# Block-sparse attention and a gated feed-forward on one core: the scores move between the two row tiles of the second product

## The chip, the core and the metric

The kernel runs on one core of one Trainium2 chip. The metric is the time of one execution on the device, in microseconds (us), as the median of several runs; lower is better. TensorE multiplies matrices and writes to PSUM; VectorE (DVE), ScalarE (ACT) and GpSimd (POOL) work elementwise; SyncE (SP) issues DMAs. Each engine takes its instructions in the order in which the program gives them.

## The reference

Inputs are q, k and v of 4 batches, 8 heads, 768 positions and head size 64, a table of three sampled key blocks for each of 24 query blocks, and two weight matrices, 512 by 2048 and back. Attention is masked by blocks of 32 positions; its output, 3072 rows of 512, goes through the feed-forward.

```python
scores = scale * np.matmul(q, k.transpose(0, 1, 3, 2))
mask = np.abs(blk_i - blk_j) <= window
mask = mask | (blk_i == 0) | (blk_j == 0) | (blk_i == n_blocks - 1) | (blk_j == n_blocks - 1)
...
scores = np.where(mask, scores, -1000000000.0)
attn = np.exp(scores - np.max(scores, axis=-1, keepdims=True))
attn = attn / (np.sum(attn, axis=-1, keepdims=True) + 1e-09)
x = np.matmul(attn, v)                      # then heads side by side: 3072 x 512
h = x @ w_in
sp = np.maximum(h, 0.0) + np.log1p(np.exp(-np.abs(h)))
g = h * erf(sp)
return g @ w_out
```

## The kernel before

Precision is kept by splitting: float32 values become two float16 halves, high and low, and a product is three float16 matmuls; the scores alone are float32 matmuls.

Attention is cut into 64 units, 16 for each batch: ten of kind "m" (a tile of four query blocks by half of the heads, with five key blocks and the sampled ones), four of kind "f" (the first and last query blocks, all keys) and two of kind "e" (the second and the one before the last query block). The feed-forward is cut into 96 groups: for each batch three chunks of two row tiles (u = 0 and 1, of 128 rows each), and for each chunk eight groups of 256 of the 2048 hidden columns.

The main loop runs over m, one step for each feed-forward group and two more. A step does, for its own group, the first product (`ff_first`, tile `h`, 24 matmuls of 128x256); for the unit two units back, where that completes a tile of rows, the values (`values`, tile `po`, 96 small matmuls, or 192 for the "f" and "e" units together); for a new unit the scores (`scores`, tiles `s_m`, `s_f`, `s_e`); and for the group two steps back the second product (`ff_second`, tile `o`, six matmuls of 128x512 for each row tile u). A table `until` spreads the 60 units left for the loop over its steps, so 60 of the 98 steps have a unit.

Around these, VectorE does `ff_gate` of the group one step back (tiles `q` and `g`), `norm` (`rinv`, `xf`), `soft_max` of the unit (the row maximum `mx`, then `nb`), `ff_power` and, late in the step, `soft_low` (`p`); ScalarE does `ff_logs` (`x`, `q`), the exponentials `soft_exp` (`pf`), `ff_exp`, and copies. `soft_turn` transposes the probabilities `p` into `pT` by a DMA in SyncE's queue; the same queue gathers the value rows (`vb`), loads queries and keys and writes results. GpSimd gathers the sampled key blocks (`keys`).

Buffers that order the work: one PSUM buffer for scores (`ps_s`), so scores of a unit wait for the exponentials of the unit before; one for `po`; three for `h`; two for `o`, so at a chunk's first group `ff_second` waits for the copies of the chunk before (`ff_store`, tile `wo<-o`: ScalarE for u = 0, VectorE for u = 1).

In the first steps the output weights are still being split into halves, by steps that short strings name (`EARLY`, `AMID`, `LATE`): `Ao` and `Bo` take a sum over the output weights for their scale (`top_wo`, then `whole_wo` on TensorE), `Ho0` and `Lo0` make the first high and low halves on ScalarE and VectorE, `Hi5` and the like those of the input weights. `EARLY[2]` is "Ao Bo Ho0 Lo0", in the step that is also the first with a second product. The scheduler keeps every engine's instructions in program order (`keep_in_program_order`). The profile gives all of them one line, L59, which is the wrapper that records them, so they are told apart by their tiles.

Of the kernel before, what the change touches and what calls it, by code (L numbers as in the profile page):

```python
# [42 lines left out]
def sparse_attention_moe(ctx: ExitStack, tc: tile.TileContext, qT, kT, v, sampled, w_in, w_out, out):  # L43
# [37 lines left out]
    FF_LAG = 2  # L81
# [25 lines left out]
    def key_blocks(b):  # L107
        return keys[:, b % 2 * (NB + 1) : (b % 2 + 1) * (NB + 1)]
# [134 lines left out]
    def write_values():  # L243
        for write in writes:
            sp.dma_start(*write)
        writes.clear()
# [318 lines left out]
    def near_keys(b, i, rows, pr):  # L565

        c = slice(pr * BLOCK, (pr + 1) * BLOCK)
        first = b % 2 * (NB + 1) + i - 1
        near = keys[rows, first : first + NR, c]
        apart = (kgs[b, i] - first) * HP * BLOCK  # L570
        return bass.AP(near.tensor, near.offset, [near.ap[0], (apart, 2), near.ap[1], near.ap[2]])
# [3 lines left out]
    def scores(unit):  # L575
        kind, b, n = unit[0], unit[1], unit[2:]
        tag = "_".join(str(x) for x in unit)
        s = ps_s.tile([P, 1024], F32, tag="s", name=f"s_{tag}")
        q = qts[b, n[0] if kind == "m" else MT]
        both = [slice(a * D, (a + 1) * D) for a in range(2)]  # L580

        def blocks_of(rows, pr, start, stop, step=1):
            return key_blocks(b)[rows, start:stop:step, pr * BLOCK : (pr + 1) * BLOCK]

        if kind == "f":
            (pr,) = n
            for c, e in ((0, 512), (512, S)):
                for rows in both:
                    k = blocks_of(rows, pr, c // BLOCK, e // BLOCK)
                    pe.matmul(s[rows, c:e], q[rows, pr, 2 * BLOCK :], k, start=True, stop=True)  # L590
            softs[unit] = (s[:, :S], 1, S)
            return
        if kind == "m":
            t, quad = n
            s4 = s.rearrange("p (a r w) -> p a r w", a=2, r=2)
            first, count, turns = 1 + 4 * t, 4, [(r, 0, s4[:, :, r]) for r in range(2)]
            softs[unit] = (s, 4, 256)
        else:
            (quad,) = n
            s3 = s.rearrange("p (a w) -> p a w", a=2)[:, :, :256]  # L600
            first, count, turns = NB - 3, 2, [(r, r * D, s3) for r in range(2)]
            softs[unit] = (s3, 2, 256)
        for r, o, out in turns:
            pr = 2 * quad + r
            for a, rows in enumerate(both):
                k = blocks_of(rows, pr, 0, NB, NB - 1)
                pe.matmul(
                    out[o : o + count * BLOCK, a, 192:], q[rows, pr, : count * BLOCK], k, start=True, stop=True
                )
        for r, o, out in turns:  # L610
            pr = 2 * quad + r
            for j in range(count):
                c = j * BLOCK
                for a, rows in enumerate(both):
                    place = out[o + c : o + c + BLOCK, a, :192]
                    near = near_keys(b, first + j, rows, pr)
                    pe.matmul(place, q[rows, pr, c : c + BLOCK], near, start=True, stop=True)
# [71 lines left out]
    CT = 2  # L689
# [14 lines left out]
    def ff_first(b, ch, fg):  # L704
        tag = f"{b}_{ch}_{fg}"
        isg = first_scale(b)
        h = ps_h.tile([P, W], F32, tag="h", name=f"h_{tag}")
        xT = xTs[b, ch].rearrange("p n u c -> p n (u c)")
        for j in range(FG):
            f = fg * FG + j  # L710
            hj = h[:, j * CW : (j + 1) * CW]
            for kt in range(NK):
                i, c = (f // 4) * NK + kt, (f % 4) * P
                hi, lo = wi16[:, i, c : c + P], wi16[:, i, 512 + c : 512 + c + P]
                xa, xb = xT[:, kt], xT[:, NK + kt]
                pe.matmul(hj, hi, xa, start=kt == 0, stop=False)
                pe.matmul(hj, hi, xb, start=False, stop=False)
                pe.matmul(hj, lo, xa, start=False, stop=kt == NK - 1)
        ffs[b, ch, fg] = (h, isg)
# [3 lines left out]
    def ff_logs(b, ch, fg):  # L723

        h, isg = ffs[b, ch, fg]
        tag = f"{b}_{ch}_{fg}"
        x = mo.tile([P, W], F32, tag="x", name=f"x_{tag}")
        act.activation(x, h, AF.Relu, bias=H_CAP, scale=isg)
        act.activation(x, x, AF.Exp, bias=H_CAP, scale=-1.0)
        act.activation(x, x, AF.Ln, bias=1.0, scale=C0)  # L730
        q = mo.tile([P, W], F32, tag="s", name=f"q_{tag}", bufs=2)
        act.activation(q, x, AF.Square, bias=C2)
        act.activation(x, x, AF.Ln, bias=1.0, scale=C4)
        ffs[b, ch, fg] = (h, x, q)
# [18 lines left out]
    def ff_second(b, ch, fg, u):  # L753
        if fg == 0:
            outs[u] = ps_o.tile([P, DM], F32, tag="o", name=f"o_{b}_{ch}_{fg}_{u}")
        g = gs[b, ch, fg]
        o = outs[u]
        for j in range(FG):
            f = fg * FG + j
            c = j * CW + u * P  # L760
            hi, lo = wo16[:, f, :512], wo16[:, f, 512:]
            pe.matmul(o, g[:, 0, c : c + P], hi, start=f == 0, stop=False)
            pe.matmul(o, g[:, 0, c : c + P], lo, start=False, stop=False)
            pe.matmul(o, g[:, 1, c : c + P], hi, start=False, stop=f == NF - 1)
# [21 lines left out]
    def write_results():  # L786
        for result in results:
            sp.dma_start(*result)
        results.clear()
# [71 lines left out]
    def seen(unit):  # L861

        if unit[0] == "m":
            return unit[1:]
        if unit[0] == "f" and unit[2] % 2 == 1:
            return unit[1], MT, unit[2] // 2
        return None

    def used_keys(unit):
        nonlocal kfree  # L870
        if unit[0] == "m" and unit[3] == 1:
            kfree += 4
        elif unit[0] == "e" and unit[2] == 1:
            kfree += 4
# [6 lines left out]
    def unit_of(n):  # L881
        return units[n] if 0 <= n < len(units) else None

    def values_of(place):
        nonlocal vfree
        values(*place)
        if place[2] == 1:
            vfree += 4 if place[1] < MT else 5
# [99 lines left out]
    groups = [(b, ch, fg) for b in range(B) for ch in range(NCH) for fg in range(NGR)]  # L988
    until = (12, 20, 25, 31, 36, 41, 47, 52, 57, 63, 67)
    for m in range(len(groups) + FF_LAG):  # L990
        ch, i = divmod(m, NGR)
        steps = 0
        if ch < len(until):
            first = until[ch - 1] if ch else FIRST
            steps = first + -(-(until[ch] - first) * (i + 1) // NGR) - begun
        elif begun < len(units) + PV_LAG:
            steps = 1
        assert steps in (0, 1)
        group = groups[m] if m < len(groups) else None
        last = groups[m - 1] if 0 < m <= len(groups) else None  # L1000
        unit = unit_of(begun) if steps else None
        old = unit_of(begun - PV_LAG) if steps else None
        place = seen(old) if old and begun - PV_LAG >= FIRST else None
        begun += steps
        write_values()
        write_results()
        if group:
            ff_first(*group)
            ff_logs(*group)
        if place:  # L1010
            values_of(place)
        if steps:
            gathers(begun)
        if unit:
            scores(unit)
            used_keys(unit)
        if last:
            ff_gate(*last)
        if place:
            norm(*place)  # L1020
        if m < len(EARLY):
            work(EARLY[m])
        if m >= FF_LAG:
            for u in range(CT):
                ff_second(*groups[m - FF_LAG], u)
        if unit:
            soft_max(unit)
            next_queries(begun - 1)
        if group:
            ff_power(*group)  # L1030
        if unit:
            soft_exp(unit)
        if group:
            ff_exp(*group)
        if m < len(AMID):
            work(AMID[m])
        if m >= FF_LAG:
            for u in range(CT):
                ff_store(*groups[m - FF_LAG], u)
        if place:  # L1040
            turn(*place)
        if unit:
            soft_low(unit)
            soft_turn(unit)
        if m < len(LATE):
            work(LATE[m])
        if unit:
            behind(begun - 1)
# [37 lines left out]
```

## Time and profile before

| | |
|---|---|
| median of 3 runs | 828.74 us (826.76 to 829.26) |
| profiled execution | 831.7 us, its span 829.9 us |
| TensorE busy | 698.5 us, 84% of the span |
| VectorE, ScalarE, GpSimd busy | 570.1, 551.3, 126.8 us |
| second product, 1152 matmuls | 385 ns each |
| mean granted clock of TensorE | 0.962 of full speed |

The profile is one execution. The loop's first step starts at about 96 us of the span, its last units' scores run near 732 us, and the rest is feed-forward alone. A busy share says how much an engine did in a stretch; what a change is worth there is told by the timeline, in which each row has the start and length of instructions that follow one another and, in brackets, how long the engine was idle before and for whom. Matmuls overlap, so the distance from one block's start to the next is used here instead of a block's own length.

### The profile page before, as it was taken

The page shows a single profiled execution, that of the slowest core. Times are in us where ns is not written, and L with a number is a line of the kernel's source. Part 1 is how long each engine was busy: PE and PEld are TensorE (multiplying, and loading weights), DVE is VectorE, ACT ScalarE, POOL GpSimd, SP SyncE. Part 2 cuts the span into 40 slices and gives each one's busy share as a digit, 9 for nine tenths or more (in the row PEclk, how much of TensorE's full clock was granted, in tenths as well). Part 3 has the DMA queues.
Part 4 walks back from the last instruction along what each step waited for, and adds up shares of the span by engine and source line. Part 5 has one row for each costly group of instructions (what it writes and reads, how often), then busy time and mean ns, then how long its engine had stood idle before and what let it go on. Part 6 is the DMA issues. An engine that isn't in the chain of part 4 may idle for free. (4 is left out here: it accounts for less than half of the span.)

```text
span 829.9 us, 26567 instructions
## 1 busy us (share of the span) xinstructions
PE 698.5 (84%) x10844; PEld 460.2 (55%) x10844; DVE 570.1 (69%) x987; ACT 551.3 (66%) x943; POOL 126.8 (15%) x343
## 2 busy tenths in 40 slices
PE   1254546888986879999999988999999999999997
PEld 1133423555654647566666556666666665666664
DVE  3994696787865666885668766876677767754454
ACT  4654567987755656776668657767677676675774
POOL 4621131002222121100103231000111110000000
PEclk9999767999998999999999999999999999999999
DMA  8999963887799898773598898752688858220000
GB/s 306 289 267 295 250 164 66 164 182 196 176 197 199 215 207 185 162 167 47 134 206 193 171 223 201 177 96 45 162 192 175 182 103 184 44 53 16 1 26 26
DMA packets 199930, 131.59 MB, mean 159 GB/s; under 512 B 144000, under 2 KB 167168, under 8 KB 199808
## 3 DMA queue, kind: packets, MB, share of 16 engines
q1 hardware_dynamic: 196384, 118.10, 62.5%
q0 software_dynamic: 3424, 11.80, 4.4%
q8 instruction: 85, 1.39, 0.7%
q14 instruction: 37, 0.30, 0.1%
HBM read 83.88 MB, written 12.95 MB: 117 GB/s over the span
## 5 line engine op out<-in xcount | busy, mean ns | idle before, releaser
L59 PE MATMUL h<-xT,wi 128*128 128x256 f16 x2304 | 275.7, 277 | 17.0 <-ACT wi L59 9.3
L59 PE MATMUL o<-wo,g 128*128 128x512 f16 x1152 | 271.4, 385 | 10.1 <-issue 3.5
L59 PEld LDWEIGHTS <-wi 128*128 128x128 f16 x2304 | 227.9, 99 | 68.7 <-ACT wi L59 10.8
L59 PEld LDWEIGHTS <-g 128*128 128x128 f16 x1152 | 109.0, 99 | 150.9 <-issue 32.4
L59 ACT ACTIVATE x<-x 128x512 f32<-128x512 f32 x288 | 181.5, 630 | 9.1
L59 POOL COPY keys<-keys 128x128 f32 x264 | 92.4, 397 | 260.1 <-PE s_m L59 173.8
L59 DVE SCALAR_TENSOR_TENSOR q<-x,q 128x512 f32<-128x512 f32 x96 | 67.8, 706 | 65.4 <-ACT x L59 65.4
L59 ACT ACTIVATE x<-h,isg 128x512 f32<-128x512 f32 x96 | 65.5, 682 | 67.7 <-PE h L59 67.6
L59 ACT ACTIVATE pf_m<-s_m,nb_m 128x256 f32<-128x256 f32 x160 | 62.6, 473 | 57.1 <-DVE nb_m L59 54.2
L59 PE MATMUL s_m<-keys,qt 64*32 64x192 f32 (+1 forms) x1600 | 71.6, 344 | 12.5 <-issue 6.1
L59 ACT ACTIVATE q<-q 128x512 f32<-128x512 f32 x96 | 60.7, 633 | 32.0 <-DVE q L59 32.0
L59 DVE SCALAR_TENSOR_TENSOR q<-q,h 128x512 f32<-128x512 f32 x96 | 65.5, 683 | 22.6 <-ACT q L59 22.6
L59 DVE SCALAR_TENSOR_TENSOR g<-q,g 128x512 f16<-128x512 f32 x96 | 66.6, 694 | 3.3
L59 PE MATMUL po<-vb,pT_m 128*32 128x65 f16 (+1 forms) x3840 | 45.8, 203 | 26.9 <-DMA vb<-vtab 15.1
L59 ACT ACTIVATE q<-x 128x512 f32<-128x512 f32 x96 | 60.5, 630 | 3.0
L59 DVE TENSOR_REDUCE mx_m<-s_m 128x4 f32<-128x1024 f32 x40 | 48.8, 1219 | 19.3 <-PE s_m L59 19.0
L59 PEld LDWEIGHTS <-pT_m 128*32 128x32 f16 x3840 | 39.0, 99 | 38.5 <-DMA vb<-vtab 16.8
L59 PEld LDWEIGHTS s_m<-keys,qt 64*32 64x32 f32 (+1 forms) x1600 | 45.2, 130 | 26.4 <-issue 9.5
L59 DVE TENSOR_TENSOR p_m<-pf_m,p_m 128x1024 f16<-128x1024 f32 x40 | 49.1, 1227 | 3.2 <-ACT p_m L59 2.2
L59 DVE TENSOR_TENSOR x<-xf,x 128x512 f16<-128x512 f32 x24 | 17.6, 734 | 38.9 <-ACT x L59 38.9
L59 DVE TENSOR_SCALAR g<-q 128x512 f16<-128x512 f32 x96 | 41.6, 433 | 3.3
L59 POOL COPY keys<-wi 128x768 f32<-128x768 f32 (+1 forms) x24 | 16.3, 705 | 163.7 <-DMA wi<-in_kT_dram 163.7
(111 smaller groups left out, 523.4 us busy)
## 6 DMA issues: line engine op xcount, KB each, us to landing
vb<-vtab SPq DMA_DIRECT2D x280, 65.0 KB, 3.3
vb<-vtab SPq DMA_DIRECT2D x32, 390.0 KB, 5.0
vraw<-in_v_dram SPq DMA_DIRECT2D x10, 768.0 KB, 5.6
vtab<-vn SPq DMA_DIRECT2D x16, 390.0 KB, 5.6
vb<-vtab SPq DMA_DIRECT2D x12, 520.0 KB, 6.1
qt<-in_qT_dram SPq DMA_DIRECT2D x20, 256.0 KB, 3.5
out_dram<-wo SPq DMA_DIRECT2D x20, 256.0 KB, 5.4
vb<-vtab SPq DMA_DIRECT2D x36, 130.0 KB, 3.3
```

The source lines that it names most:

```text
L59: done = call(*args, **kwargs)
```

## The change

The call of `scores` and the note that its keys are used move from the place before `ff_gate` and `norm` to a place between the two row tiles of the second product.

```diff
         if steps:
             gathers(begun)
-        if unit:
-            scores(unit)
-            used_keys(unit)
         if last:
             ff_gate(*last)
         if place:
             norm(*place)
         if m < len(EARLY):
             work(EARLY[m])
         if m >= FF_LAG:
-            for u in range(CT):
-                ff_second(*groups[m - FF_LAG], u)
+            ff_second(*groups[m - FF_LAG], 0)
+        if unit:
+            scores(unit)
+            used_keys(unit)
+        if m >= FF_LAG:
+            ff_second(*groups[m - FF_LAG], 1)
         if unit:
             soft_max(unit)
```

Only TensorE's order changes. In the first step with a second product (m = 2), TensorE has before this, where `s_m_3_0` are the scores of unit ("m", batch 0, tile 3, first half of the heads), `whole_wo` is the sum over the output weights, and `o_0_0_0` and `o_0_0_1` are the accumulators of the two row tiles:

```order
L59 MATMUL po_2_0_1365<-vb,pT_m_2_0_1225 32x65
L59 MATMUL s_m_3_0_1474<-keys,qt_3_1147 128x64 x4
L59 MATMUL s_m_3_0_1474<-keys,qt_3_1147 32x192 x16
L59 MATMUL whole_wo<-one,top_wo 128x1
L59 LDWEIGHTS g_0_0_1292
L59 MATMUL o_0_0_0_1518<-wo,g_0_0_1292 128x512
```

and now, in the same place:

```order
L59 MATMUL po_2_0_1365<-vb,pT_m_2_0_1225 32x65
L59 MATMUL whole_wo<-one,top_wo 128x1
L59 LDWEIGHTS g_0_0_1271
L59 MATMUL o_0_0_0_1497<-wo,g_0_0_1271 128x512
...
L59 MATMUL s_m_3_0_1504<-keys,qt_3_1147 128x64 x4
L59 MATMUL s_m_3_0_1504<-keys,qt_3_1147 32x192 x16
L59 LDWEIGHTS g_0_0_1271
L59 MATMUL o_0_0_1_1525<-wo,g_0_0_1271 128x512
```

The scores stand behind the sum and behind the first row tile of the second product. On VectorE, which reads these scores (`mx_m_3_0`), the same place reads now:

```order
L59 TENSOR_REDUCE top_wo<-sums 128x1
L59 TENSOR_SCALAR m_wo<-whole_wo 128x1
...
L59 SCALAR_TENSOR_TENSOR wo<-wo,s_wo 128x2x512
L59 TENSOR_REDUCE mx_m_3_0_1532<-s_m_3_0_1504 128x4
L59 TENSOR_SCALAR nb_m_3_0_1534<-mx_m_3_0_1532 128x4
```

Nothing moved there: the order is that of before, with the new tile's number.

At the first group of the second batch's first chunk, where the accumulators must have been copied out, TensorE (with buffer numbers; `s_e_1_0` are the scores of unit ("e", batch 1, first half)) has before:

```order
L59 MATMUL po_1_4_1_5575<-vb_88,pT_m_1_4_1_5349 32x65
L59 MATMUL s_e_1_0_5673<-keys_85,qt_1_5_4818 64x64 x4
L59 MATMUL s_e_1_0_5673<-keys_85,qt_1_5_4818 32x192 x8
L59 LDWEIGHTS g_1_0_0_5499
L59 MATMUL o_1_0_0_0_5694<-wo_102,g_1_0_0_5499 128x512
```

and now:

```order
L59 LDWEIGHTS g_1_0_0_5494
L59 MATMUL o_1_0_0_0_5681<-wo_102,g_1_0_0_5494 128x512
L59 MATMUL s_e_1_0_5688<-keys_85,qt_1_5_4818 64x64 x4
L59 MATMUL s_e_1_0_5688<-keys_85,qt_1_5_4818 32x192 x8
L59 LDWEIGHTS g_1_0_0_5494
L59 MATMUL o_1_0_0_1_5701<-wo_102,g_1_0_0_5494 128x512
```

The scores no longer stand between the values and the first matmul that needs a free accumulator.

## Rows read from the trace of the kernel before

**Rows 1.** The page's engine line: busy us, share of the span, instructions.

```profile
PE 698.5 (84%) x10844; PEld 460.2 (55%) x10844; DVE 570.1 (69%) x987; ACT 551.3 (66%) x943; POOL 126.8 (15%) x343
```

**Rows 2.** Windows: us, busy time and count by engine, granted clock, DMA share, GB/s.

```profile
100.00:200.00 100.00, 70.53 (x1116) 43.29 (x1115) 80.13 (x124) 77.17 (x125) 16.25 (x39) 0.83 0.69 157
...
600.00:700.00 100.00, 97.78 (x1702) 66.60 (x1701) 75.62 (x136) 71.37 (x128) 12.31 (x42) 1.00 0.81 172
...
131.00:135.00 4.00, 3.27 (x9) 1.13 (x8) 2.72 (x4) 1.72 (x5) 0.00 (x0) 0.50 0.00 0
```

**Rows 3.** Timeline of PE: start us, length us, line, operation, tiles, count.

```profile
569.27 2.78 PE L59 MATMUL h<-xT,wi 128*128 128x256 f16 x24
571.98 1.47 PE L59 MATMUL s_m<-keys,qt 64*128 64x64 f32 x40
573.39 2.76 PE L59 MATMUL o<-wo,g 128*128 128x512 f16 x12
575.99 2.78 PE L59 MATMUL h<-xT,wi 128*128 128x256 f16 x24
578.61 1.67 PE L59 MATMUL o<-wo,g 128*128 128x512 f16 x7
```

**Rows 4.** Timeline of PE, a step that also has values.

```profile
594.24 1.10 PE L59 MATMUL po<-vb,pT_m 128*32 128x65 f16 x96
595.26 1.47 PE L59 MATMUL s_m<-keys,qt 64*128 64x64 f32 x40
```

**Rows 5.** Timeline of PE around the sum of the output weights.

```profile
114.92 1.47 PE L59 MATMUL s_m<-keys,qt 64*128 64x64 f32 x40
...
130.55 0.59 PE L59 MATMUL o<-wo,g 128*128 128x512 f16 x1 [2.31 <-ACT wo L59]
131.87 4.16 PE L59 MATMUL o<-wo,g 128*128 128x512 f16 x11 [0.73 <-DVE wo L59]
...
147.17 0.39 PE L59 MATMUL h<-xT,wi 128*128 128x256 f16 x2 [2.87 <-ACT wi L59]
```

**Rows 6.** Timelines of DVE and ACT in the same stretch.

```profile
131.74 1.22 DVE L59 TENSOR_REDUCE mx_m<-s_m 128x4 f32<-128x1024 f32 x1
...
133.25 1.56 ACT L59 ACTIVATE pf_m<-s_m,nb_m 128x256 f32<-128x256 f32 x4 [2.75 <-DVE nb_m L59]
...
145.98 1.13 ACT L59 ACTIVATE wi<-wi,s_wi 128x1024 f16<-128x1024 f32 x1
```

**Rows 7.** Timeline of PE, two scores that wait for exponentials.

```profile
188.02 1.51 PE L59 MATMUL s_f<-keys,qt 64*64 64x512 f32 x8 [0.82 <-ACT pf_e L59]
...
195.53 1.51 PE L59 MATMUL s_f<-keys,qt 64*64 64x512 f32 x8 [0.69 <-ACT pf_f L59]
```

**Rows 8.** Timelines at two chunk ends: values, and the copy of an accumulator.

```profile
347.00 0.96 PE L59 MATMUL po<-vb,pT_m 128*32 128x65 f16 x96 [1.22 <-DMA pT_m<-p_m]
...
348.54 0.68 ACT L59 ACTIVATE wo<-o,iso 128x512 f32<-128x512 f32 x1
...
525.46 1.03 PE L59 MATMUL po<-vb,pT_m 128*32 128x65 f16 x96
...
526.68 0.68 ACT L59 ACTIVATE wo<-o,iso 128x512 f32<-128x512 f32 x1
```

**Rows 9.** A late transpose in the timeline; PE's waits for gathers, 100 to 780 us.

```profile
685.79 4.60 SPq L59 DMA_TRANSPOSE pT_m<-p_m  x1
...
692.52 1.10 PE L59 MATMUL po<-vb,pT_m 128*32 128x65 f16 x96 [1.69 <-DMA pT_m<-p_m]
...
PE po L59 <- DMA vb<-vtab: 5.9, 6, 3.4
```

**Rows 10.** PE's waits at scores, 100 to 780 us: total, times, longest us.

```profile
PE s_m L59 <- issue: 6.1, 5, 2.4
...
PE s_f L59 <- ACT pf_m L59: 1.9, 1, 1.9
...
PE s_m L59 <- POOL keys L59: 1.7, 4, 0.7
```

## The prediction

> **What bounds the kernel now.** I read the page's engine line first [rows 1]: TensorE is busy 84% of the span, every other compute engine 69% or less, so the question is where TensorE is idle and why. The windows [rows 2] divide the run. From 100 to 200 us TensorE is busy 70.53 of 100 us while VectorE (DVE) has 80.13 and ScalarE (ACT) 77.17: the weights are still being split, and those two engines set the pace. From 600 to 700 us TensorE is busy 97.78 of 100: there its own work is the bound. A change of TensorE's order is therefore worth different things in the two stretches.
>
> An undisturbed step is a sequence of blocks, each read by its start. A first product followed by the second product lasts 578.61 − 575.99 = 2.62 us; followed by scores it lasts 571.98 − 569.27 = 2.71 us [rows 3]. Scores take 573.39 − 571.98 = 1.41 us, a second product 575.99 − 573.39 = 2.60 us, half of it 1.30 us [rows 3]. Values take 595.26 − 594.24 = 1.02 us and go straight to scores [rows 4].
>
> **The change part by part.** Nothing is added or removed; on VectorE, ScalarE, GpSimd and the DMA queues the order is the same. On TensorE, 58 of the 60 score blocks of the main loop move behind six matmuls of the second product (the first two steps have none yet), and 43 of the 58 stand in a step that also has values.
>
> *A, the step with the sum of the output weights.* Here TensorE does the scores at 114.92 and then stands, but for the small product of the sum, until 130.55 and 131.87 us, when ScalarE has the high half and VectorE the low half of the weights [rows 5]. So the scores are hidden in the wait today. In the new order they stand behind the first six matmuls of the second product, which are what waits. [...] Five of these end the first half at about 133.8 us; the scores then take 1.41 us if the clock is up and at most twice that, so they end at 135.2 to 136.6 us. The row maximum that reads them began at 131.74 us and was not held by them; now it starts 3.5 to 4.9 us later, and I take 4.4, since the clock was still at 0.50 up to 135 us. Behind it everything is in line: ScalarE already waits 2.75 us for its result at 133.25 us, then works through its list up to the weight split at 145.98 us, and TensorE waits for that split at 147.17 us, 2.87 us [rows 5, 6]. In between ScalarE waits once more, but for VectorE, which is itself behind the same row maximum; so nothing takes up the shift, and it arrives whole: +4.4 us.
>
> *The part of A that comes back.* At 188.02 and 195.53 us scores wait 0.82 and 0.69 us for exponentials that ScalarE is late with, since the score buffer is single [rows 7]. In the new order TensorE has 1.3 us of second product to do in each place first, and both waits go. They are separate waits for one late ScalarE, so I count 1.0 of the 1.5 us. A nets +3.4 us, between +0.5 (the shift only costs TensorE the 1.41 us of scores, less 1.0) and +5.
>
> *B, one more change of tile shape.* Leaving 128*128 tiles for scores costs 2.71 − 2.62 = 0.09 us [rows 3]. A step without values has two such changes before and after. A step with values goes values, scores, second product today and values, second product, scores, second product afterwards: one more. 43 × 0.09 = 3.9 us of TensorE time. It costs only where TensorE is the bound; about 20 of the 43 steps lie in such stretches (350 to 410 and from 530 us), so +1.8 us, bounds 0 and 3.9. [...]
>
> *C, waits that the scores used to cover.* The first half of the second product now stands where the scores stood, 1 us earlier, and waits for what it needs. At 347.00 us values of 0.96 us start; the result copy that frees the accumulator begins at 348.54 and takes 0.68, to 349.22 us [rows 8]. Today scores fill that time; afterwards TensorE waits 349.2 − 348.0 = 1.2 us and does the scores later: +1.0. The same pattern stands at 525.46, where the copy ends at 527.36 us [rows 8]: +0.9, from which I take 0.6 for the wait of 1.9 us on exponentials at 517 us [rows 10], whose gain stops at values that are nearly late themselves. C is +1.3 us, bounds 0 and 3.
>
> *D, later probabilities.* Scores start 1.3 us later relative to the values and the first product. Row maximum, exponentials, split and transposing DMA follow. The DMA queue in SyncE takes them in line: the transpose at 685.79 us issues for 4.60 us, and values wait 1.69 us for it at 692.52 us [rows 9]. The later scores lengthen this by 1.2 us. In the stretch from 240 to 265 us the gathers of values queue behind such transposes, and TensorE waits up to 3.4 us for them [rows 9]: another 1.3 us. Elsewhere the row maximum is late for reasons of VectorE, or the transposed tile is there some us early. D is +2.5 us, bounds 0 and 6.
>
> *E, gains.* Five times scores stand still with no releaser shown, 6.1 us in all [rows 10]; they follow a dense run of small matmuls, so six large ones in between give whatever is late 1.1 to 1.3 us more. At most 5 us; but those before 480 us are followed by waits on VectorE or DMA that do not move, so I count 1.0 us. The waits on key copies, 1.7 us in four, likewise lie ahead of such waits [rows 10] and count as nothing. E is −1.0 us, bounds 0 and −6.
>
> Sum: 3.4 + 1.8 + 1.3 + 2.5 − 1.0 = +8.0 us. The profiled execution took 831.7 us (span 829.9), 3.0 above the median of 828.74, so 839.7 in its terms and **836.7 us** against the median.
>
> **The rivals.** *The covers count* (faster). Every wait in front of scores is real time of TensorE, and 1.3 us of second product hides up to 1.3 us of each: 5 us of the unexplained ones, 1.5 at 188 and 195, 1.3 at 517 and 1.7 on keys, together 9.5 us [rows 7, 10]. Against them stand B's 3.9 and A's 1.4 of scores alone. 828.7 − 9.5 + 5.3 = 824.5 us. It decides from the point at which later waits for DMA and VectorE shrink by what TensorE gained; the wait of 1.69 us for a transposed tile [rows 9] speaks against it, since an earlier TensorE only waits longer there.
>
> *A is absorbed* (about no change). If ScalarE's list has slack, A costs 0.5 and D, with most transposed tiles early, 0.5: 0.5 + 1.8 + 1.3 + 0.5 − 2.0 = +2.1, 830.8 us. The wait for the weight split at 147.17 speaks against it [rows 5].
>
> *Each late transpose counts* (much slower). If the loop from scores over the transposing DMA and the value gathers back to values is the bound in more of the middle than the two places of D, every one of some five places pays 1.3 us: +6.5 more, less what B then hides (0.9): 836.7 + 5.6 = 842.3 us. The SyncE queue's long issues speak for it [rows 9], the 97.78 of 100 us against it for the late part [rows 2].
>
> **How the numbers follow.** Forecast 0.57; much slower 0.14; absorbed 0.17; covers count 0.12. Something like 0.3%, 2.5 us, is what a measurement of this kernel tells from no change, that is 826.2 to 831.2 us. Forecast and much slower lie above it but for 0.04; of absorbed 0.06 lies above and 0.11 within; of covers count 0.08 lies below, 0.04 within. That gives slower 0.73, same 0.19, faster 0.08. The range leaves out the faster rival and the upper part of the slowest: 828.5 to 843.0 us.
>
> **What would show it.** In the changed profile the row maximum after the sum of the output weights starts 3.5 to 5 us later after that sum than now, and TensorE's next wait for a weight split ends about 4.4 us later (A). A step from 600 to 700 us with values is 0.09 us longer between its waits (B). TensorE waits for the result copy directly after values near 350 and 530 us (C), and longer for the transposed tile near 695 us (D). Fewer pauses stand inside score blocks (E). If the time at which TensorE passes the first product after 200 us is not about 3 us later, A is wrong; if the wait near 695 us has not grown, D is.

## The result, and the profile after

The changed kernel took 837.34 us (median of 6 runs, 833.57 to 840.84) against 829.0 us of the kernel before beside it: ratio 1.011, with an interval of 1.0072 to 1.0147. It is slower, by 8.3 us. A second set on another chip gave 1.012 (1.0074 to 1.0167). The forecast was 836.7 us.

The profiled execution took 835.43 us (span 833.7). It is 1.9 us under the median where that of before was 3 us above its own, so the two traces stand only 3.7 us apart; sizes below are therefore taken from the medians of the experiments, and the traces tell places. First the page's engine line and two windows of the kernel after, as in [rows 1] and [rows 2]:

```profile
PE 698.7 (84%) x10844; PEld 453.9 (54%) x10844; DVE 567.1 (68%) x987; ACT 550.2 (66%) x943; POOL 128.1 (15%) x343
```

```profile
100.00:200.00 100.00, 69.58 (x1060) 41.27 (x1061) 77.52 (x123) 75.62 (x122) 16.81 (x36) 0.78 0.63 149
600.00:700.00 100.00, 97.60 (x1725) 64.98 (x1725) 75.73 (x138) 69.26 (x125) 12.31 (x42) 1.00 0.79 166
```

Busy times hardly move, as they should when only an order changes. The change is in what TensorE waits for. Timelines of the kernel after around the sum of the output weights (PE, then DVE, then ACT), which answer to [rows 5] and [rows 6]:

```profile
126.32 0.59 PE L59 MATMUL whole_wo<-one,top_wo 128*128 128x1 f32 x2 [12.95 <-DVE top_wo L59]
129.22 0.58 PE L59 MATMUL o<-wo,g 128*128 128x512 f16 x1 [2.31 <-ACT wo L59]
130.54 2.29 PE L59 MATMUL o<-wo,g 128*128 128x512 f16 x5 [0.74 <-DVE wo L59]
132.76 2.58 PE L59 MATMUL s_m<-keys,qt 64*128 64x64 f32 x40
...
142.28 0.38 PE L59 MATMUL o<-wo,g 128*128 128x512 f16 x1 [1.46 <-ACT wo L59]
143.76 2.29 PE L59 MATMUL o<-wo,g 128*128 128x512 f16 x5 [1.10 <-DVE wo L59]
```

```profile
135.45 1.23 DVE L59 TENSOR_REDUCE mx_m<-s_m 128x4 f32<-128x1024 f32 x1 [4.96 <-PE s_m L59]
```

```profile
136.98 1.57 ACT L59 ACTIVATE pf_m<-s_m,nb_m 128x256 f32<-128x256 f32 x4 [7.81 <-DVE nb_m L59]
...
149.67 1.14 ACT L59 ACTIVATE wi<-wi,s_wi 128x1024 f16<-128x1024 f32 x1
```

The scores at 132.76 us now come behind the two waits for the output weights, and take 2.58 us instead of 1.47 [rows 5], because the granted clock is still 0.50 there (window of 132.8 to 135.2 us). VectorE waits 4.96 us for them, ScalarE 7.81 us instead of 2.75.

Further on, PE's waits from 200 to 780 us in the kernel after (total us, times, longest), beside [rows 9] and [rows 10]:

```profile
PE po L59 <- DMA pT_m<-p_m: 11.1, 6, 3.0
PE po L59 <- DMA vb<-vtab: 8.3, 7, 5.0
PE po L59 <- issue: 4.8, 3, 1.7
PE s_m L59 <- issue: 2.9, 4, 1.3
PE o L59 <- DVE g L59: 2.6, 4, 1.2
PE h L59 <- DVE m_v L59: 2.5, 2, 1.5
PE o L59 <- DVE wo L59: 1.9, 2, 1.0
PE o L59 <- DVE q L59: 1.6, 1, 1.6
PE o L59 <- issue: 1.4, 1, 1.4
PE s_m L59 <- POOL keys L59: 0.2, 1, 0.2
```

The same answer for the kernel before begins with `pT_m` at 6.4 in 4, has 0.3 us for `g`, 0.3 for `o <- ACT wo`, and nothing for `o <- DVE wo`. Grouped by the block that waits, with the pauses that have no releaser put to their block except those in values; two columns are kernels of the next section, "start doubled" with the order of before in this whole stretch and "middle" with the new order in it up to m = 51:

| 200 to 780 us | before | start doubled | after | after, other chip | middle |
|---|---|---|---|---|---|
| values, for DMA | 12.3 | 14.5 | 19.4 | 22.4 | 14.6 |
| values, no releaser | 5.1 | 3.8 | 4.8 | 3.3 | 4.8 |
| scores | 10.3 | 11.4 | 3.1 | 3.1 | 4.2 |
| second product | 5.6 | 6.9 | 7.5 | 8.1 | 10.3 |
| first product | 2.2 | 2.5 | 2.5 | 3.0 | 2.3 |
| sum | 35.5 | 39.1 | 37.3 | 39.9 | 36.2 |

The waits in front of scores fell by 7.2 us, and those of values for DMA grew by 7.1 us in this trace. Each column is one execution: two with the same order in this stretch differ by 3.6 us in their sums (35.5 and 39.1), so these sums do not show the loss of the middle. What stands out is the fall at scores in all three kernels with the new order, and that it comes back at different blocks: at values in the kernel after, at the second product in the middle kernel. The clock does not tell the orders apart: the mean granted clock from 200 to 780 us is 0.99 before and after, and 0.98 in the second set, in the middle kernel and in five steps, which takes no longer than before.

### The profile page after: what moved, and what is told of

Same layout as the page of the kernel before. It is cut to its first block, busy times and chain, and to the rows that moved or that the text cites. A ratio compares the mean times of both kernels' runs of the same rounds, so it can differ in the third digit from the quotient of the medians.

```text
span 833.7 us, 26566 instructions
## 1 busy us (share of the span) xinstructions
PE 698.7 (84%) x10844; PEld 453.9 (54%) x10844; DVE 567.1 (68%) x987; ACT 550.2 (66%) x943; POOL 128.1 (15%) x343
## 3 DMA queue, kind: packets, MB, share of 16 engines
q8 instruction: 85, 1.39, 0.7%
## 5 line engine op out<-in xcount | busy, mean ns | idle before, releaser
L59 PE MATMUL o<-wo,g 128*128 128x512 f16 x1152 | 283.4, 387 | 16.4 <-DVE wo L59 5.0
L59 PE MATMUL h<-xT,wi 128*128 128x256 f16 x2304 | 274.1, 276 | 14.7 <-ACT wi L59 7.2
L59 PEld LDWEIGHTS <-g 128*128 128x128 f16 x1152 | 105.1, 99 | 147.3 <-issue 39.3
L59 PE MATMUL s_m<-keys,qt 64*32 64x192 f32 (+1 forms) x1600 | 69.3, 347 | 7.6 <-ACT pf_m L59 4.1
```

The costliest lines, as they stand in the source:

```text
L59: done = call(*args, **kwargs)
```

## The experiments

Each kernel was timed in five rounds beside the kernel before on the same chip; on those chips the kernel before took 833.2 to 833.7 us, so the ratios carry over and not the microseconds. 0.1% is 0.83 us.

| kernel | new order in | ratio (interval) |
|---|---|---|
| start only | m = 2 | 1.0045 (1.0017 to 1.0073) |
| start doubled | m = 2, behind both row tiles | 1.0068 (1.0039 to 1.0097) |
| middle | m = 0, 1, 3 to 51 | 1.0060 (1.0032 to 1.0088) |
| late only | m from 52 | 1.0004 (0.9984 to 1.0024) |
| no start | all but m = 2 | 1.0047 (1.0026 to 1.0068) |
| two chunk starts alone | m = 26, 50 | 1.0019 (0.9996 to 1.0042) |
| chunk starts undone | all but m = 10, 18, 26 and so on | 1.0067 (1.0045 to 1.0089) |
| values moved along | most of m = 3 on | 1.0113 (1.0086 to 1.0141) |
| five steps | m = 8, 9, 19, 44, 49 | 1.0003 (0.9978 to 1.0028) |
| scores first, four | none; the other way at 4 steps | 1.0015 (0.9987 to 1.0043) |
| scores first, all | none; the other way | 1.0103 (1.0067 to 1.0139) |
| changed kernel again | all | 1.0120 (1.0074 to 1.0167) |

Start, middle and late add to 0.45 + 0.60 + 0.04 = 1.09%, and the whole is 1.1 to 1.2%.

**The changed kernel again.**

> The changed kernel once more, beside the three below on one chip. Theory (the parts add): the step m = 2 alone gave +0.45% and all other steps +0.47%, so +0.9%, about 7.6 us above the kernel before. Rival (the parts help each other along, a later start shifting every transfer behind it): 1.2% or more.

It gave 1.012, the lower end of the rival, with an interval that holds the theory's +0.9% too. Start, middle and late together account for 1.09%, so nothing asks for an effect of one part on another, though a small one is not excluded.

**The start.** The edit that all kernels with the new order at some steps share: scores ahead of the second product where the condition holds, and between its row tiles elsewhere.

```
+        ahead = m == 2            # start only: m != 2
+        if unit and ahead:
+            scores(unit)
+            used_keys(unit)
...
-        if unit:
+        if unit and not ahead:
             scores(unit)
             used_keys(unit)
```

> The changed kernel with one step put back: at m = 2 (unit 6, where the second product begins) the scores stand ahead of the second product again, every other step keeps the new order. Theory: the row maximum of unit 6 ends about 4 us after the sum of the output scale again, not 9.1 us, the first product of step 7 starts 4 to 5 us sooner than in the changed kernel, and 3.4 to 4.5 us of that reach the end: about 833 us, still 4 us above the kernel before. Rival (the late start is absorbed, the 8 us come from the other 56 steps): 837 us, as the changed kernel.

> The kernel before with one step changed: only at m = 2 the scores stand between the two row tiles of the second product, every other step has the old order. Theory: the row maximum of unit 6 ends 5 us later after the sum of the output scale, the wait for the weight split that follows does too, and about 1 to 2 us come back where a wait on probabilities near 190 us gets shorter: 832 to 833 us against 829. Rival (absorbed): within 1 us of the kernel before.

Start only gave 1.0045, 3.7 us, no start 1.0047, 3.9 us: each takes about half of the loss, and both rivals (837 us for the one, no change for the other) fall. In the trace of start only, the sum stands at 126.78 us, then (DVE, ACT, PE):

```profile
135.92 1.23 DVE L59 TENSOR_REDUCE mx_m<-s_m 128x4 f32<-128x1024 f32 x1 [4.96 <-PE s_m L59]
```

```profile
150.17 1.13 ACT L59 ACTIVATE wi<-wi,s_wi 128x1024 f16<-128x1024 f32 x1
```

```profile
151.36 0.61 PE L59 MATMUL h<-xT,wi 128*128 128x256 f16 x2 [3.93 <-ACT wi L59]
```

The row maximum comes 135.92 − 126.78 = 9.14 us after the sum; before it was 131.74 − 127.65 = 4.09 us, and with no start it is 132.35 − 128.25 = 4.10 us. The weight split comes 23.39 us after the sum instead of 18.33. So 5.05 us enter at the row maximum and 5.06 arrive at ScalarE's split: the chain takes up nothing. TensorE's wait for it is 3.93 us, from 2.87 [rows 5]. From the first product of m = 2 to that of m = 8 start only takes 3.5 us more than the kernel before. In the kernel after, the first product of m = 11, the first behind 200 us in the kernel before (211.65 us), starts at 213.70 us: 2.0 us later on the clock of the trace and 3.4 us later counted from the sum.

**The start doubled.** The kernel before with, at m = 2 alone:

```
             for u in range(CT):
                 ff_second(*groups[m - FF_LAG], u)
+        if unit and behind_both:  # m == 2
+            scores(unit)
+            used_keys(unit)
```

> The kernel before with one step changed, m = 2, whose scores now stand behind both row tiles of the second product instead of between them: the shift of the step m = 2 of the change doubled. Theory (the row maximum of unit 6 carries its delay to the weight split): the row maximum ends 2.5 to 4 us later again than with the step m = 2 alone, and the time is 1.5 to 3 us above that one's +0.45%: +0.65 to +0.8%. Rival (what costs is the wait of TensorE that is no longer filled, and that is lost already): +0.45% again.

1.0068, inside the theory's 0.65 to 0.8%, but its interval still holds the rival's 0.45%. The row maximum was expected 2.5 to 4 us later than with the single shift and came only 0.9 us later (137.04 − 126.99 = 10.05 us after the sum). The windows of this kernel tell why (131.3 to 133.3 us, and the scores at 135.5):

```profile
131.30:133.30 2.00, 2.00 (x5) 0.61 (x5) 0.00 (x0) 0.00 (x0) 0.00 (x0) 0.50 0.00 0
...
135.50:136.80 1.30, 1.30 (x41) 0.97 (x40) 0.00 (x0) 0.00 (x0) 0.00 (x0) 1.00 0.00 0
```

By then TensorE had run eleven matmuls in 4.31 us without a gap and the granted clock had risen from 0.50 to 1.00, so that the scores took 1.47 us and not 2.58. A shift twice as large in blocks was not twice as large in time. So the theory's number is met, but not by its way: TensorE's own waits for weight halves at m = 3 are 3.1 us here (1.92 and 1.21) where start only has 0.95. This kernel does not decide between the two.

**Middle and late.** The same edit with `ahead = m == 2 or m >= 52`, and with `ahead = m < 52`.

> The kernel before with the new order only at m = 0, 1 and 3 to 51. Theory: this is where the part that is not the start sits, two waits of the second product's first row tile on the result copy (1 and 2 us net), on exponents of the group two back (about 1 to 2 us in three places), less about 1 to 2 us of waits of scores that go: +3 us. Rival (all of it is in the late stretch): within 1 us of the kernel before.

> The kernel before with the new order only from m = 52 on, the stretch that TensorE fills. Theory: 0.1 us of extra tile change in each of about ten steps with values, one or two waits of values on transposed probabilities that grow by up to 1 us, and one pause inside scores of 0.9 us that goes: between 0 and +1.5 us. Rival (late probabilities count in full where nothing else limits): +3 us or more.

The middle carries +0.60%, 5.0 us (interval 2.7 to 7.3), more than the 3 expected; the late stretch +0.04%, 0.3 us, the low end of what was expected, and the rival's +3 us is out by a good deal. The late steps do show the extra change of tile shape: in the no-start trace the first product comes 0.11, 0.12, 0.10 and 0.11 us later, against the trace before, at m = 65, 71, 73 and 79, each behind a step with values and scores. There are thirteen such steps from m = 52 on, so at most 1.4 us, and a pause of 0.82 us inside scores near 588 us, of which 0.17 us is left in late only, pays for part of it.

**The chunk starts.** The same edit with `ahead = m not in (26, 50)`; and all undone but m = 2, with `ahead = m > 2 and groups[m - FF_LAG][2] == 0`. A chunk has eight groups, so the second takes m = 10, 18, 26, 34 and so on; but by the table `until` only m = 10, 26, 50 and 74 of these have scores, so it puts back four steps. The first takes the two of them where a wait had been read; its text below speaks as if no other start had scores, which is not so for m = 10 and 74.

> The kernel before with the new order at two steps only, m = 26 and 50, the first of a chunk's second product that have scores. Theory: there the scores covered the copy of the last chunk's results; the second product now waits about 1 us at each, and the middle steps' +0.6% hold +0.2 to +0.4% of it: 2 to 3 us above the kernel before. Rival (each wait only stands in for one on transposed probabilities or on exponents of scores that would have come anyway): within 1 us of the kernel before.

> The changed kernel with the old order in the first step of each chunk's second product (after m = 2), where its first row tile writes the accumulators that the result copies read; all other steps as in the changed kernel. Theory: the waits of the second product on the copies at 349.55 us (0.94 us) and 529.61 us (1.11 us) go, and the time falls by 1 to 2 us, to 835 to 836 us. Rival (the copies only stand in for another wait that then takes their place): within 0.5 us of the changed kernel.

In the trace of the kernel after, first row tiles wait at both chunk starts right behind values (PE; then the two copies at the first, DVE and ACT):

```profile
347.72 0.96 PE L59 MATMUL po<-vb,pT_m 128*32 128x65 f16 x96 [1.75 <-DMA pT_m<-p_m]
349.55 1.46 PE L59 MATMUL o<-wo,g 128*128 128x512 f16 x6 [0.87 <-DVE wo L59]
...
527.61 0.96 PE L59 MATMUL po<-vb,pT_m 128*32 128x65 f16 x96 [1.57 <-DMA pT_m<-p_m]
529.61 2.72 PE L59 MATMUL o<-wo,g 128*128 128x512 f16 x6 [1.04 <-DVE wo L59]
```

```profile
348.75 0.75 DVE L59 TENSOR_SCALAR wo<-o,iso 128x512 f32<-128x512 f32 x1
349.21 0.68 ACT L59 ACTIVATE wo<-o,iso 128x512 f32<-128x512 f32 x1
```

The row tile at 349.55 us starts when VectorE's copy has ended (349.50 us) and while ScalarE's still runs (to 349.89 us), so here it waits for the copy that VectorE makes; with two chunk starts alone, the tile at m = 26 starts at 350.49 us, behind ScalarE's copy (to 350.44 us). At m = 50 a second cost stands beside the wait: TensorE has stood 1.57 and 1.04 us, the granted clock is 0.50 from 529.6 to 532.2 us, and the row tile lasts 2.65 us by the starts instead of 1.39 at m = 26. The traces of two chunk starts (2.65 us) and of no start show the same there, those of the middle kernel and of the second set do not.

Alone the two steps cost 0.19%, 1.6 us, which falls between the theory's 2 to 3 us and the rival's 1, and the interval reaches just under no change. With all starts undone the changed kernel gives back 0.4 to 0.5% (1.0067 against 1.011 and 1.012), about 4 us, more than the 1 to 2 expected, and the two waits are gone from its trace. What m = 10 and 74 add is not seen: no trace with the new order there has a wait of the second product for a copy at either. The difference of two ratios is no finer than some 3 us.

**Values moved along.** From m = 3 on, but for the first step of each chunk, the first row tile goes ahead of the values:

```
+        moved = m > 2 and groups[m - FF_LAG][2] != 0
+        if moved:
+            ff_second(*groups[m - FF_LAG], 0)
         if place:
             values_of(place)
...
+        if unit and moved:
+            scores(unit)
+            used_keys(unit)
         if m >= FF_LAG:
             ff_second(*groups[m - FF_LAG], 1)
```

> The scores stand between the row tiles of the second product as in the changed kernel, but the values are moved with them: first product, first row tile, values, scores, second row tile. The step m = 2 and the first step of each chunk keep the old order. So a step has one change of tile shape as before, the transposed probabilities have the slack they had or more, and the copy of results at the chunk's start is met as before. Theory (the loss comes from the start, the extra tile change and the chunk starts, not from late scores as such): late steps with values lose their 0.10 us, and the time is 826 to 829 us, the kernel before or a little under it. Rival (scores that come about 1.3 us later in the step cost time by themselves, through the softmax and what waits behind it): 832 us or more.

The theory fell: 1.0113, as slow as the changed kernel, though the start and the chunk starts are as before and the extra tile change is gone (the steps behind m = 79 and 85 last exactly as before, to 0.05 us). The rival's number is met, but the waits show a cause neither had named. PE's waits of this kernel, 200 to 780 us:

```profile
PE o L59 <- DVE g L59: 9.7, 7, 3.1
```

`g` is the gated hidden tile that the second product reads, written by VectorE for the group two back. The wait for it is 0.3 us in the kernel before, where values and scores stand ahead of the second product; 2.6 us after, and 4.4, 4.2 and 4.7 us in the second set, in no start and in the middle kernel, where only values do; and 9.7 us here, where nothing does. The steps are not as clean as these numbers: with the order of before in this stretch, start only has 0.2 and start doubled 2.2 us. One place is at 331 us in the kernel after (PE, DVE):

```profile
328.92 0.96 PE L59 MATMUL po<-vb,pT_m 128*32 128x65 f16 x96
331.04 1.76 PE L59 MATMUL o<-wo,g 128*128 128x512 f16 x6 [1.16 <-DVE g L59]
332.74 1.47 PE L59 MATMUL s_m<-keys,qt 64*128 64x64 f32 x40
```

```profile
330.56 0.43 DVE L59 TENSOR_SCALAR g<-q 128x512 f16<-128x512 f32 x1
```

and the same place in the kernel before (PE, DVE):

```profile
331.28 1.47 PE L59 MATMUL s_m<-keys,qt 64*128 64x64 f32 x40
```

```profile
330.33 0.69 DVE L59 SCALAR_TENSOR_TENSOR g<-q,g 128x512 f16<-128x512 f32 x1
```

In the kernel before both halves of `g` are there at 331.02 us, before the values end at 331.3 us, so the scores covered nothing at this place. In the kernel after TensorE comes to these values 1.47 us earlier, and VectorE writes `g` 0.69 us later. Had the scores, 1.40 us, still stood behind the values, the row tile would have started at about 331.2 us (an estimate from these rows), behind the first half of `g` at 330.99. So the wait needs both: a block of cover less, and a TensorE that is early.

**Five steps, chosen for their waits.** The same edit with `ahead = m not in (8, 9, 19, 44, 49)`.

> The kernel before with the new order only at five steps, m = 8, 9, 19, 44 and 49: those whose scores wait in the trace of the kernel before on probabilities (0.82, 0.69 and 1.95 us) or on rounded keys (0.72 and 0.76 us), 4.9 us together. Theory: the waits go, the first row tile covers them, half comes back as later waits on transposed probabilities: 2 to 4 us under the kernel before. Rival (the waits move from run to run, and what a step gains, the next one waits for): within 1 us of the kernel before.

1.0003: the rival. At m = 49 the wait is seen to move. The kernel before (PE):

```profile
517.06 2.44 PE L59 MATMUL s_f<-keys,qt 64*64 64x512 f32 x8 [1.95 <-ACT pf_m L59]
...
525.46 1.03 PE L59 MATMUL po<-vb,pT_m 128*32 128x65 f16 x96
```

and five steps:

```profile
514.45 1.51 PE L59 MATMUL s_f<-keys,qt 64*64 64x512 f32 x8 [0.56 <-ACT pf_m L59]
...
522.37 0.96 PE L59 MATMUL po<-vb,pT_m 128*32 128x65 f16 x96 [2.40 <-DMA pT_m<-p_m]
```

The scores gain 1.39 us, and the next values wait 2.40 us for a transposed tile that used to be there. Over 200 to 780 us the waits at scores fall from 10.3 to 6.2 us here, those of values for DMA rise from 12.3 to 19.9; with the order of before they are 12.3 to 14.5.

**The other way: scores ahead of values.** At four steps, and in all from m = 3 on:

```
+        if unit and early:        # m in (20, 26, 44, 74); or m > 2
+            scores(unit)
+            used_keys(unit)
         if place:
             values_of(place)
```

> The kernel before with the scores put ahead of the values, the other way than the change moves them, at four steps (m = 20, 26, 44 and 74) whose values wait 1.6, 1.3, 2.0 and 1.7 us on transposed probabilities in the trace of the kernel before. Theory (scores are cover for the wait of whatever stands behind them): the waits, 6.6 us together, go under 2.6 to 5.2 us of scores, and 3 to 6 us of it reach the end: 0.4 to 0.7% under the kernel before. Rival (scores then wait themselves for the last unit's exponents, or the next values wait instead): within 1 us of the kernel before.

> The kernel before with the scores ahead of the values in every step from m = 3 on. Theory of cover: the waits of values on transposed probabilities and on gathered value rows go in the whole stretch (12 us in the trace of the kernel before), some waits of scores on exponents and keys come for them (5 us there now): 3 to 7 us under the kernel before. Rival (scores that come earlier by the values' length wait for the last unit's exponents in most steps): 2 us or more above it.

Neither gains. With four steps the waits of values for `pT_m` do fall, from 6.4 to 1.6 us, but waits for `g` come for them, from 0.3 to 5.6 us, though the scores still stand ahead of the second product in every step, and at 343.52 us the scores themselves wait 2.43 us for exponentials: 1.0015. With all steps it is 1.0103, the rival. PE's waits there, 200 to 780 us:

```profile
PE po L59 <- issue: 11.5, 9, 2.5
PE s_e L59 <- ACT pf_f L59: 6.3, 3, 3.2
...
PE s_f L59 <- ACT pf_m L59: 5.4, 2, 2.8
PE s_m L59 <- ACT pf_m L59: 3.9, 3, 1.5
```

Scores that come earlier wait 15.6 us for ScalarE, which still reads the last unit's scores from the single buffer. So the order of before lies between two that are both about 1% slower, and no kernel here beats it.

## Why the prediction was right, point by point

The time and the sign were right. Of the five terms A holds, but for the part that was to come back; B holds as a price and is small as a term; C holds in kind and misses the waits for `g`; D and E were each far too small in their waits and nearly cancel.

**A, the start: right.** Forecast +4.4 us at the row maximum and +3.4 at the end, measured 5.05 and 3.7 (interval 1.4 to 6.1). The row maximum was later than 4.4, and a little later than the upper end given, 4.9, because the scores ran wholly at the 0.50 clock: five matmuls and the scores took 2.22 and 2.52 us by their starts in the kernel after, where the forecast, with the five done at about 133.8 us, has 1.9 us for them (by the 4.16 us of eleven in [rows 5]) and 1.41 to 2.82 for the scores (by the clock of 0.50 in [rows 2]). The way there, through ScalarE's list to the weight split with nothing taken up, is what start only shows, and its rival, absorbed, is out. In the full change m = 3 adds a little: its first row tile stands ahead of its scores too and waits 1.46 and 1.10 us for weight halves at 142.28 and 143.76 us, where start only waits 0.95 in all. The waits at 188 and 195 us went, as said; one of 0.83 us for a weight half came at 192.43 us. The 1.0 us that was to come back there is not shown. It belongs to m = 8 and 9, which start only leaves in the old order, so its 3.7 us stands beside the forecast 4.4 and not beside 3.4. From the first product of m = 7 to that of m = 10 the kernel before takes 22.39 us, the kernel after 21.84 and five steps, which has both, 22.59: 0.5 us gained or none.

**B, the tile change: right as a price, small as a term.** 0.10 to 0.12 us a step is seen where nothing else limits, and 0.09 had been read from [rows 3]. But the late kernel, with all of its late steps, comes to +0.3 us net, so there less arrives than was counted; what the 29 such steps of the middle pay is not measured by itself. The kernel after, PE, beside [rows 4]:

```profile
597.91 0.90 PE L59 MATMUL po<-vb,pT_m 128*32 128x65 f16 x89 [0.40 <-DMA vb<-vtab]
598.74 1.47 PE L59 MATMUL o<-wo,g 128*128 128x512 f16 x6
600.14 1.47 PE L59 MATMUL s_m<-keys,qt 64*128 64x64 f32 x40
601.55 1.47 PE L59 MATMUL o<-wo,g 128*128 128x512 f16 x6
602.85 1.36 PE L59 MATMUL h<-xT,wi 128*128 128x256 f16 x11
```

By the starts the first row tile, followed by scores, lasts 1.40 us and the second, followed by a first product, 1.30: the 0.10 us stands where large tiles give way to the scores' small ones.

**C, lost cover: seen in the traces, the list of places too short.** The two result copies were forecast at +1.3 us and cost 1.6 alone, but the interval, −0.3 to 3.5, holds nothing too. The waits are there, 0.87 and 1.04 us where 1.2 and 0.9 were read ahead; the prediction took the copy for ScalarE's, and in the kernel after it is VectorE's. In the trace of the two steps alone the lower clock at m = 50 adds another 1.25 us (2.65 − 1.40), which the prediction did not have, so that the size is in part luck. Not foreseen was the wait for `g`: I had looked at what the second product needs only where a chunk begins, and taken `g`, which never delayed anything in the trace before beyond 0.3 us, for early. It adds 2.3 us of waits in the trace after, about 4 in the others; that part of this is lost cover and part a gain of E given back is read from the place at 331 us and not separated by a run.

**D, later probabilities: right in kind, wrong in place and size.** By its own test it failed: the wait near 695 us did not grow but fell from 1.69 to 0.80 us. There the transposing DMA took 3.54 us to issue where it had taken 4.60. The waits for transposed tiles as a whole went from 6.4 to 11.1 us, at other places. A late one (kernel after, SyncE's queue and PE):

```profile
647.25 1.24 SPq L59 DMA_TRANSPOSE xT<-x  x1
648.58 3.07 SPq L59 DMA_TRANSPOSE pT_m<-p_m  x1
...
653.71 1.04 PE L59 MATMUL po<-vb,pT_m 128*32 128x65 f16 x96 [1.60 <-DMA pT_m<-p_m]
```

The tile's probabilities were written by 642.66 us; the transpose stood in the queue behind gathers and another transpose until 648.58. In the kernel before the same wait in the queue was 4.3 us and the tile came in time.

**E, gains: far too small, and given back.** Forecast −1.0; waits at scores fell by 7.2 us, the pauses without a releaser from 6.1 to 2.9, the rest nearly whole. But five steps shows that such a gain is not kept: its time is that of before, and values then wait for the transposed tile. So D and E act as one term, which is argued from these traces: a wait taken away in front of one block stands again in front of a later one, at values in the kernel after and in five steps, at the second product in the middle kernel, where values wait 14.6 us for DMA as with the order of before. Forecast +1.5 for the two together, the trace has −0.1 at these two blocks. That is also the answer to the faster rival, which counted each wait in front of scores as TensorE's own time: it named the point that decides, and the runs are on the other side of it.

Together, without the start: forecast 4.6 us, measured 3.9 (no start, 2.2 to 5.7) and 5.0 in the middle. That the terms met the sum is in part luck: C was short by about what D and E together were over.

Open is how the middle's 0.60% splits between the copies, `g`, the tile change and what is left of D after E. No kernel was run that changes the wait for `g` alone, so its price is read from waits in traces and from the values-moved kernel, not measured by itself.

## What to carry to other kernels

A block that never waits may be the one that hides somebody's wait: before moving it, list everything that the block then first in line needs, at every step, and the margin by which it is ready (here the waits for `g`, up to 2.2 us with the order of before, were 2.6 to 4.7 with one block of cover gone and 9.7 with two). A wait in front of a block is a gain to be had only if what comes next in the same loop is early; test it at the few steps with the longest waits first (at m = 49 of five steps the scores gained 1.39 us and the next values waited 2.40). And where one engine's wait starts a serial chain, as at the sum of the output weights, work that hides in that wait is free exactly because it stands there (moved out of it, the scores cost 3.7 us in start only).

## What was not expected of the hardware

The pauses on TensorE without a releaser come behind packets of one DMA queue, named instruction. The page counts, for the kernel before (queue, packets, MB, share of the DMA engines):

```profile
q8 instruction: 85, 1.39, 0.7%
```

1.39 MB in 85 packets is 16 KB each. TensorE has 10844 matmuls and as many weight loads, 21688 instructions, which would be 255 to a packet, an estimate from these counts that takes the queue for TensorE's alone; whose instructions it carries is not shown. In the window of 409 to 412.5 us one such packet ends at 410.52 us, and the scores, which had stopped after 24 of 40, go on at 411.83 us:

```profile
409.48 1.15 PE L59 MATMUL s_m<-keys,qt 64*128 64x64 f32 x24
411.83 0.56 PE L59 MATMUL s_m<-keys,qt 64*32 64x192 f32 x16 [1.20 <-issue]
```

Near 588 and 629 us it is the same, packets that end at 586.70 and 628.35 us and pauses that end 1.41 and 1.38 us later. Of the kernel before all ten pauses without a releaser between 200 and 780 us, 14.7 us together, end 1.31 to 1.55 us after the end of such a packet, while the 69 packets that end in this stretch come 8.4 us apart on the mean. The pauses follow dense runs of small matmuls (96 or 192 of values, with or without scores). With scores ahead of values in all steps, none is listed in scores and 11.5 us in nine stand in values, so the place seems to follow the run of small instructions and not the data. That TensorE's instructions are late there is read from these coincidences; no kernel here was made to test it.
